# Second layer's weight conversions spread evenly over two tiles, and products with x's high parts before those with its low parts in a tile's first step

## The chip, the core and the metric

The kernel runs on one core of a Trainium2 chip. The metric is the device time of one execution in microseconds (us). Engines: PE is TensorE's matmul, PEld its weight load, DVE is VectorE, ACT is ScalarE, POOL is GpSimd, SP is SyncE, whose queue issues most DMAs.

## The reference

A delta-rule attention over 768 tokens (4 x 8 heads of 48) gives x, 3072 tokens of 384 features. Two feed-forward layers follow, and they are most of the work:

```python
x = attn_out.transpose(0, 2, 1, 3).reshape(3072, 384)
h = x @ w1_in                      # 384 -> 2048
g = h * (1 / (1 + exp(-1.702 * h)))
x = g @ w1_out                     # 2048 -> 384
h = maximum(x @ w2_in, 0)          # 384 -> 2048
out = (h * h) @ w2_out             # 2048 -> 384
```

The weights arrive as float64. The kernel turns them into float32 itself.

## The kernel before

**Tiles and steps.** Each layer runs over six tiles of 512 tokens; a tile is written here as (layer, j), from (1,0) to (2,5). In a tile, 16 steps f = 0 to 15 each take 128 of the 2048 hidden features. `step(ph, j, f)` issues the products into one of two PSUM banks h0 and h1 in turn, for three chunks c of x's 384 features, then ACT's tanh (or relu), DVE's product g, ACT's ghi and DVE's glo. `layer2` issues the products of the step before into three banks z0 to z2. So PE does nine 128x512 products into h and nine into z in a step.

**High and low parts.** PE works here on a float32r type, so every operand is a pair: hi, and lo = value - hi. A product is three: hi·hi, hi·lo and lo·hi. `split_x` makes x_hi on ACT and x_lo on DVE when a tile begins. Layer 1 has one pair of x buffers, so x_hi of tile j+1 may only be written when step 15 of tile j has been through its h products.

**Conversions.** `split_w` turns one chunk (128 x 384 float64, one f of one matrix) into hi and lo: ACT makes c0 from raw, DVE does two TENSOR_SCALAR into c1 (two buffers) and one SCALAR_TENSOR_TENSOR, ACT copies hi, and POOL subtracts lo = c1 - hi (`tt` with two queues: DVE where the planner finds it sooner). `load_w` brings the float64 into one of three raw buffers. The second layer has 32 chunks: 16 of w2_in into vi_hi and vi_lo, 16 of w2_out into wo_hi and wo_lo, in the place of the first layer's, so chunk f of those may only be written when `layer2` of (1,5) and f has been done.

**What sets the order.** `Program.add` records operations with costs; `flush` plans them with a cost table, engine by engine, and emits them in the planned order. From then on each engine runs its queue in order and waits on semaphores. There are two flushes: one up to the end of tile (1,4) with the attention, one for (1,5) and layer 2. In the attention, between the steps of layer 1, DVE also runs transposes (gu from G, kT_sb from gu), a product Td, and some fifteen small operations on 128x32 tiles named sm_.

Of the kernel before, what the change touches and what calls it, by code (L numbers as in the profile page):

```python
# [22 lines left out]
KX = 3  # L23
NF = DFF // 128
NT = B * S
CT = B * C
TT = 512
EPS = 1e-6
GATE = 1.702
TUNE = dict(  # L30
    fused=4,
    warm=(10, 6),
    burst=(6, 4, 220),
    blocks=(0, 1, 2, 3),
    ja=4,
    depth=2,
    half=8,
    slack=0.0,
# [12 lines left out]
class Program:  # L51
# [8 lines left out]
    def __init__(self, queues):  # L60
        self.queues = queues
        self.ops = []
        self.writer, self.readers = {}, {}
        self.free = {q: 0.0 for q in queues}
        self.dma_free = 0.0
        self.urgent = False
        self.columns = {}
        self.run = self.run_end = self.burst_end = 0.0

    def add(self, queue, cost, fn, reads=(), writes=(), early=0, nbytes=0, after=(), cold=None):  # L70
        n = len(self.ops)
        deps = set(after)
        for k in reads:
            if k in self.writer:
                deps.add(self.writer[k])
        for k in writes:
            if k in self.writer:
                deps.add(self.writer[k])
            deps.update(self.readers.get(k, ()))
        for k in reads:  # L80
            self.readers.setdefault(k, []).append(n)
        for k in writes:
            self.writer[k], self.readers[k] = n, []
        queue = (queue,) if isinstance(queue, str) else queue
        cost = cost if isinstance(cost, tuple) else (cost,)
        self.ops.append([queue, cost, fn, deps, n - early, nbytes, None, self.urgent, cold])
# [102 lines left out]
def kernel(  # L189
# [14 lines left out]
    w1_in, w1_out, w2_in, w2_out = (w.bitcast(I32) for w in (w1_in, w1_out, w2_in, w2_out))  # L204
    pg = Program({"pe": nc.tensor, "act": nc.scalar, "dve": nc.vector, "pool": nc.gpsimd, "sp": nc.sync})
# [8 lines left out]
    h_ps = [psum.tile([128, TT], F32, name=f"h{i}") for i in range(2)]  # L214
# [8 lines left out]
    wo_hi = main.tile([128, NF, DM], F32R, name="wo_hi")  # L223
    wo_lo = main.tile([128, NF, DM], F32R, name="wo_lo")
# [7 lines left out]
    NR = 3  # L232
# [33 lines left out]
    def act(n, reads, writes, early=0, **kw):  # L266
        kw.setdefault("func", AF.Copy)
        pg.add("act", c_act(n), lambda e: e.activation(**kw), reads, writes, early)  # L268
# [11 lines left out]
    def tt(n, reads, writes, out, in0, in1, op, queue="dve", early=0):  # L280
        cost = {"dve": c_dve(n), "pool": c_pool(n)}
        cost = cost[queue] if isinstance(queue, str) else tuple(cost[q] for q in queue)
        pg.add(queue, cost, lambda e: e.tensor_tensor(out=out, in0=in0, in1=in1, op=op), reads, writes, early)  # L283
# [5 lines left out]
    def stt(n, reads, writes, early=0, **kw):  # L289
        pg.add("dve", c_dve(n), lambda e: e.scalar_tensor_tensor(**kw), reads, writes, early)  # L290
# [4 lines left out]
    def mms(cost, todo, reads, writes, density=1.0):  # L295
        if not isinstance(cost, tuple):
            cost = cost, 2 * cost
        def fn(e):
            for out, lhsT, rhs, start, stop in todo:
                e.matmul(out=out, lhsT=lhsT, rhs=rhs, start=start, stop=stop)  # L300
        pg.add("pe", cost[0], fn, reads, writes, cold=(cost[1], 2400 * cost[0] * density))
# [4 lines left out]
    def load_w(src, f):  # L306
        s = n_conv[0] % NR
        n_conv[0] += 1
        dma(raw_sb[s], src[:, f].rearrange("p (n two) -> p n two", two=2), [], [("raw", s)], 128 * DM * 8)
# [27 lines left out]
    def halves_of(c0, n):  # L337
        return [x for x in range(2) if c0 <= x * CT < c0 + n]
# [362 lines left out]
    def layer2(ph, j, f, c0, n, hi, lo, K):  # L701
        for e in range(KX):
            ps = z_ps[e][:, c0:c0 + n]
            wh = wo_hi[:, f, 128 * e:128 * e + 128]
            wl = wo_lo[:, f, 128 * e:128 * e + 128]
            first, last = f == 0 and c0 == 0, f == NF - 1
            mms(3 * 0.000423 * n, [(ps, wh, hi, first, False), (ps, wh, lo, False, False), (ps, wl, hi, False, last)],
                [("wo", f, 0), ("wo", f, 1)] + K, [("z", e)])
        if f == NF - 1:
            dst = zd if ph == 1 else out  # L710
            for e in range(KX):
                key, zs = zs_of[ns[1] % NR]
                ns[1] += 1
                act(TT, [("z", e)], [key], out=zs, in_=z_ps[e], scale=0.5 if ph == 1 else 1.0)
                dma(dst[128 * e:128 * e + 128, TT * j:TT * j + TT], zs, [key],
                    [("zd", j, e)] if ph == 1 else [], 128 * TT * 4)

    def step(ph, j, f, c0=0, n=TT, b=0, mid=()):
        p = ns[0] % 2
        ns[0] += 1  # L720
        parts = range(2)
        if n == TT:
            ns[2] += ns[2] % 2
            s, o = ns[2] // 2 % NG, 0
            ns[2] += 2
        else:
            s, o = ns[2] // 2 % NG, CT * (ns[2] % 2)
            parts = [ns[2] % 2]
            ns[2] += 1
        W, halves = ("wi", "vi")[ph - 1], halves_of(c0, n)  # L730
        ps = h_ps[p][:, :n]
        for c in range(KX):
            wh = w_in_of[ph][0][:, f, 128 * c:128 * c + 128]
            wl = w_in_of[ph][1][:, f, 128 * c:128 * c + 128]
            hi, lo = x_hi[b][:, c, c0:c0 + n], x_lo[b][:, c, c0:c0 + n]
            mms(3 * 0.000423 * n, [(ps, wh, hi, c == 0, False), (ps, wh, lo, False, False), (ps, wl, hi, False, c == KX - 1)],
                [(W, f, 0), (W, f, 1)] + [("x", b, c, half, i) for half in halves for i in range(2)], [("h", p)])
        for todo in mid:
            todo()
        g, hi, lo = (x[s][:, o:o + n] for x in (g_sb, ghi_sb, glo_sb))  # L740
        kg, khi, klo = ([(x, s, i) for i in parts] for x in ("g", "ghi", "glo"))
        if ph == 1:
            act(n, [("h", p)], kg, out=g, in_=ps, func=AF.Tanh, scale=GATE / 2)
            stt(n, [("h", p)] + kg, kg, out=g, in0=g, scalar=1.0, in1=ps, op0=ALU.add, op1=ALU.mult)
        else:
            act(n, [("h", p)], kg, out=g, in_=ps, func=AF.Relu)
            tt(n, [("h", p)] + kg, kg, g, g, ps, ALU.mult)
        act(n, kg, khi, out=hi, in_=g)
        tt(n, kg + khi, klo, lo, g, hi, ALU.subtract)
        prev.append((ph, j, f, c0, n, hi, lo, khi + klo))  # L750
        while len(prev) > (1 if n == TT else TUNE["depth"]):
            layer2(*prev.pop(0))
# [5 lines left out]
    def convert(todo, load, n, key=None):  # L758
        for _ in range(n):
            if todo:  # L760
                _, key, f, hi, lo = todo.pop(0)
                split_w(key, f, hi, lo)
            if load:
                load_w(*(load[0][0], load.pop(0)[2]))

    with tc.manual_schedule():
# [111 lines left out]
        vi_hi = p2.tile([128, NF, DM], F32R, name="vi_hi")  # L878
        vi_lo = p2.tile([128, NF, DM], F32R, name="vi_lo")
# [6 lines left out]
        def load_z(j):  # L886
            for c in range(KX):
                dma(xf_sb[:, c], zd[128 * c:128 * c + 128, TT * j:TT * j + TT], [("zd", j, c)], xf_keys(c, 0, TT), 128 * TT * 4)

        w2i = [(w2_in, "vi", f, vi_hi, vi_lo) for f in range(NF)]  # L890
        w2o = [(w2_out, "wo", f, wo_hi, wo_lo) for f in range(NF)]
        ni, no = list(w2i), list(w2o)
        convert([], ni, NR)
        for f in range(NF):
            if f == 2:
                load_z(0)
            step(1, 5, f)
            convert(w2i, ni, 1)
        for key in [("x", 1, c, half, 1) for c in range(KX) for half in range(2)]:
            pg.readers[key] = [r for k in x_lo_keys for r in pg.readers.get(k, [])]  # L900
        split_x(1, 0, TT)
        while w2i:
            convert(w2i, ni, 1)
        for j in range(6):
            for f in range(NF):
                step(2, j, f, b=(j + 1) % 2)
                if j == 0:
                    if f == 0:
                        convert([], no, NR)
                    convert(w2o, no, 1)  # L910
                if f == 1 and j < 5:
                    load_z(j + 1)
                if f == 12 and j < 5:
                    split_x(j % 2, 0, TT)
# [69 lines left out]
```

## Time and profile before

| | us |
|---|---|
| median of 3 runs (lowest, highest) | 1086.88 (1084.77, 1090.79) |
| the profiled execution | 1084.37 |
| its span | 1082.7 |
| busy in it: PE, DVE, ACT, POOL | 1024.4, 589.6, 528.5, 332.9 |

The span runs from the first to the last instruction of the program in the profile; 1.7 us of the execution lie around it. Busy time of PE is a poor measure of its work, since matmuls overlap; the count of products in a stretch tells more. At full pace 128x512 products start 0.227 us apart. Layer 2 ends the span, and PE has no pause in most of it.

### The profile page before, as it was taken

The numbers are of one execution on the slowest core, as the hardware profiler recorded it, in microseconds if no ns is written. First come the engines' busy times: TensorE is split into PE (matmuls) and PEld (weight loads), VectorE is DVE, ScalarE is ACT, GpSimd is POOL, SyncE is SP. The second block draws the span as 40 slices with busy tenths as digits, with TensorE's granted clock in tenths as the row PEclk, the third lists the DMA queues.
The fourth block names the chain that finished last, engine by engine and source line by source line (L and its number), as shares of the span: only waits on it lengthen the run. The fifth ranks groups of instructions, "written<-read, shape, count | busy, mean of one in ns | idle before, by whom it ended". The sixth has DMA issues, their size and how long they took to land.

```text
span 1082.7 us, 23994 instructions
## 1 busy us (share of the span) xinstructions
PE 1024.4 (95%) x9900; PEld 832.9 (77%) x9900; DVE 589.6 (54%) x1122; ACT 528.5 (49%) x1088; POOL 332.9 (31%) x673
## 2 busy tenths in 40 slices
PE   4789899999999999999999989999999999999998
PEld 3778777867778787878788867788888888888886
DVE  6787886574655546453744799634333343433332
ACT  4586675636464546455544656534233242332323
POOL 1254251786647382847280144100000000000000
PEclk7798999999999999999999999999999999999999
DMA  8364462313223122212110566201001010000000
GB/s 225 98 170 133 139 174 61 113 31 93 57 60 101 60 56 88 64 51 73 50 34 5 172 179 169 94 0 59 1 7 53 1 59 1 1 30 1 30 1 29
DMA packets 43981, 76.32 MB, mean 70 GB/s; under 512 B 6624, under 2 KB 19552, under 8 KB 43872
## 3 DMA queue, kind: packets, MB, share of 16 engines
q1 hardware_dynamic: 43776, 74.75, 23.6%
q8 instruction: 77, 1.26, 0.5%
q14 instruction: 32, 0.26, 0.1%
q10 hardware_dynamic: 96, 0.05, 0.0%
HBM read 64.16 MB, written 9.44 MB: 68 GB/s over the span
## 4 chain that ended last, share of the span: by engine, by line
PE 66%; DVE 16%; ACT 8%; issue 4%; POOL 3%; DMA 2%; SPq 1%; DVEq 0%; ACTq 0%; POOLq 0%
PE h L300 28%; PE z L300 28%; PE a L300 9%; DVE c L287 3%; ACT G L273 3%; DVE kT_sb L293 2%; DVE glo L283 2%; DVE c L290 2%; DVE gu L293 1%; DVE g L290 1%; POOL tmpp L544 1%; DVE v_sb L283 1%; POOL U L547 1%; ACT gu L268 1%; DVE x_lo L283 1%
## 5 line engine op out<-in xcount | busy, mean ns | idle before, releaser
L268 ACT ACTIVATE g<-h 128x512 f32<-128x512 f32 (+1 forms) x200 | 115.5, 579 | 266.0 <-PE h L300 264.7
L300 PE MATMUL z<-glo,wo_hi 128*128 128x512 f32 (+1 forms) x600 | 231.8, 386 | 5.6 <-DVE glo L283 5.6
L300 PE MATMUL z<-ghi,wo_hi 128*128 128x512 f32 (+1 forms) x600 | 232.0, 387 | 0.1
L300 PE MATMUL z<-ghi,wo_lo 128*128 128x512 f32 (+1 forms) x600 | 229.7, 383 | 0.0
L283 DVE TENSOR_TENSOR glo<-g,ghi 128x512 fp32r<-128x512 f32 (+1 forms) x200 | 137.7, 689 | 98.6 <-ACT ghi L268 98.0
L268 ACT ACTIVATE ghi<-g 128x512 fp32r<-128x512 f32 (+1 forms) x200 | 122.6, 614 | 134.4 <-DVE g L290 68.5
L283 DVE TENSOR_TENSOR g<-g,h 128x512 f32<-128x512 f32 x96 | 66.1, 688 | 172.4 <-ACT g L268 172.4
L300 PE MATMUL h<-x_hi,wi_hi 128*128 128x512 f32 (+1 forms) x312 | 129.9, 416 | 18.3 <-DVE g L290 15.1
L544 POOL TENSOR_TENSOR tmpp<-U,gu 128x126 f32<-128x126 f32 (+22 forms) x248 | 113.2, 457 | 95.8 <-DVE U L287 77.0
L300 PEld LDWEIGHTS z<-glo,wo_hi 128*128 128x128 f32 x600 | 113.7, 189 | 33.2 <-DVE glo L283 11.8
L300 PEld LDWEIGHTS z<-ghi,wo_hi 128*128 128x128 f32 x600 | 113.6, 189 | 24.0 <-ACT ghi L268 0.9
L300 PEld LDWEIGHTS z<-ghi,wo_lo 128*128 128x128 f32 x600 | 113.7, 190 | 21.5
L290 DVE SCALAR_TENSOR_TENSOR g<-g,h 128x512 f32<-128x512 f32 (+1 forms) x104 | 66.5, 640 | 105.1 <-ACT g L268 104.9
L300 PE MATMUL h<-x_lo,wi_hi 128*128 128x512 f32 (+1 forms) x312 | 118.8, 381 | 3.2 <-DVE x_lo L283 3.2
L300 PE MATMUL h<-x_hi,wi_lo 128*128 128x512 f32 (+1 forms) x312 | 118.7, 380 | 0.4 <-DVE wi_lo L283 0.4
L300 PE MATMUL h<-x_hi,vi_hi 128*128 128x512 f32 x288 | 112.4, 390 | 0.8 <-PE h L300 0.8
L300 PE MATMUL h<-x_hi,vi_lo 128*128 128x512 f32 x288 | 112.2, 390 | 0.0
L547 POOL TENSOR_TENSOR U<-U,tmpp 128x126 f32<-128x126 f32 (+22 forms) x248 | 102.8, 415 | 20.4 <-DVE U L287 1.3
L300 PEld LDWEIGHTS h<-x_hi,wi_hi 128*128 128x128 f32 x312 | 59.7, 191 | 42.3 <-DVE g L290 24.7
L300 PEld LDWEIGHTS h<-x_hi,wi_lo 128*128 128x128 f32 x312 | 60.0, 192 | 11.6 <-DVE wi_lo L283 0.6
L300 PEld LDWEIGHTS h<-x_lo,wi_hi 128*128 128x128 f32 x312 | 60.1, 192 | 11.2 <-DVE x_lo L283 4.4
L273 ACT ACTIVATE ws<-a 32x384 f32<-32x384 f32 x92 | 44.3, 482 | 49.6 <-PE a L300 45.2
(117 smaller groups left out, 1451.4 us busy)
## 6 DMA issues: line engine op xcount, KB each, us to landing
raw<-in_w_in SPq DMA_DIRECT2D x32, 384.0 KB, 3.5
raw<-in_w_out SPq DMA_DIRECT2D x32, 384.0 KB, 3.4
kq<-in_kq SPq DMA_DIRECT2D x44, 256.0 KB, 3.0
kT_sb<-in_kq SPq DMA_DIRECT2D x11, 512.0 KB, 3.7
k_sb<-in_kt SPq DMA_DIRECT2D x12, 384.0 KB, 4.5
v_sb<-in_vt SPq DMA_DIRECT2D x12, 384.0 KB, 3.2
xf_sb<-zd SPq DMA_DIRECT2D x18, 256.0 KB, 2.7
out<-zs SPq DMA_DIRECT2D x18, 256.0 KB, 2.0
```

The source lines that it names most:

```text
L268: pg.add("act", c_act(n), lambda e: e.activation(**kw), reads, writes, early)
L273: e.activation(out=out, in_=in_, func=AF.Copy)
L283: pg.add(queue, cost, lambda e: e.tensor_tensor(out=out, in0=in0, in1=in1, op=op), reads, writes, early)
L287: pg.add("dve", c_dve(n, True), lambda e: e.tensor_scalar(**kw), reads, writes, early)
L290: pg.add("dve", c_dve(n), lambda e: e.scalar_tensor_tensor(**kw), reads, writes, early)
L293: pg.add("dve", c_dve(n), lambda e: e.transpose(out=out, in_=in_), reads, writes)
L300: e.matmul(out=out, lhsT=lhsT, rhs=rhs, start=start, stop=stop)
L544: e.tensor_tensor(out=t, in0=U[:, lo:hi, j:j + 1].to_broadcast(shape), in1=gu[:, j + 1:, j:j + 1].rearrange("p i o -> p o i").to_broadcast ...
L547: e.tensor_tensor(out=U[:, lo:hi, j + 1:], in0=U[:, lo:hi, j + 1:], in1=t, op=ALU.add)
```

## The change

Three edits. First, the lists of chunks: before, all 16 chunks of w2_in stood behind the steps of (1,5), one by one, and all 16 of w2_out behind those of (2,0). Now one list takes them in turns, vi 0, wo 0, vi 1, and so on. Second, a gate: chunk f of w2_in is held in the plan until step int(1.8 f), counted from the first step of (1,5), has been planned, that of w2_out two steps later. A gate is a dependency for the planner alone; it adds no wait on the chip. Third, in step 0 of the tiles (1,1) to (1,5) the six products with x_hi stand first, for all three chunks, and the three with x_lo after them, each as an operation of its own.

```diff
     def add(self, queue, cost, fn, reads=(), writes=(), ...):
         n = len(self.ops)
-        deps = set(after)
+        deps = set(after) | set(self.gate)
...
         for c in range(KX):
...
+            if ph == 1 and f == 0 and n == TT:
+                K = [("x", b, c, half, 0) for half in halves]
+                mms(2 * 0.000423 * n, [(ps, wh, hi, c == 0, False), (ps, wl, hi, False, False)], [(W, f, 0), (W, f, 1)] + K, [("h", p)])
+                late.append((c, wh, lo))
+                continue
...
+        for c, wh, lo in late:
+            mms(0.000423 * n, [(ps, wh, lo, False, c == KX - 1)], [(W, f, 0)] + [("x", b, c, half, 1) for half in halves], [("h", p)])
...
-        w2i = [(w2_in, "vi", f, vi_hi, vi_lo) for f in range(NF)]
-        w2o = [(w2_out, "wo", f, wo_hi, wo_lo) for f in range(NF)]
-        ni, no = list(w2i), list(w2o)
-        convert([], ni, NR)
+        w2 = [x for f in range(NF) for x in ((w2_in, "vi", f, vi_hi, vi_lo), (w2_out, "wo", f, wo_hi, wo_lo))]
+        w2_load = list(w2)
+        starts = []
+
+        def spread():
+            starts.append(len(pg.ops) - 1)
+            while w2:
+                at = int(TUNE["spread"] * w2[0][2]) + 2 * (w2[0][1] == "wo")
+                if at >= len(starts):
+                    break
+                pg.gate = starts[at:at + 1]
+                convert(w2, (), 1)
+                pg.gate = ()
+                convert((), w2_load, 1)
+
+        convert([], w2_load, NR)
         for f in range(NF):
             if f == 2:
                 load_z(0)
             step(1, 5, f)
-            convert(w2i, ni, 1)
+            spread()
...
-        while w2i:
-            convert(w2i, ni, 1)
         for j in range(6):
             for f in range(NF):
                 step(2, j, f, b=(j + 1) % 2)
                 if j == 0:
-                    if f == 0:
-                        convert([], no, NR)
-                    convert(w2o, no, 1)
+                    spread()
```

**DVE in the two tiles.** Names: g0, g1 and glo0, glo1 are the two buffers of a step's g and lo part, c10 and c11 the two buffers of a conversion, x_lo0 the low part of the next tile's x. Before, this stood for a step near the end of (1,5):

```order
L290 SCALAR_TENSOR_TENSOR g0_82<-g0_82,h0_67 128x512
L290 SCALAR_TENSOR_TENSOR c10_92<-c00_91,c10_92 128x384
L283 TENSOR_TENSOR glo0_86<-g0_82,ghi0_84 128x512
L287 TENSOR_SCALAR c11_93<-raw0_88 128x384 x2
L290 SCALAR_TENSOR_TENSOR c11_93<-c00_91,c11_93 128x384
L287 TENSOR_SCALAR c10_92<-raw1_89 128x384 x2
L290 SCALAR_TENSOR_TENSOR g1_83<-g1_83,h1_68 128x512
```

Two conversions lie between one g and the next. Now two conversions share two steps in most places, as here in (2,0):

```order
L285 TENSOR_TENSOR g1_83<-g1_83,h1_68 128x512
L289 TENSOR_SCALAR c11_93<-raw1_89 128x384
L285 TENSOR_TENSOR glo1_87<-g1_83,ghi1_85 128x512
L289 TENSOR_SCALAR c11_93<-raw1_89 128x384
L289 TENSOR_SCALAR c10_92<-raw2_90 128x384
L292 SCALAR_TENSOR_TENSOR c11_93<-c00_91,c11_93 128x384
L289 TENSOR_SCALAR c10_92<-raw2_90 128x384
L285 TENSOR_TENSOR g0_82<-g0_82,h0_67 128x512
L292 SCALAR_TENSOR_TENSOR c10_92<-c00_91,c10_92 128x384
L285 TENSOR_TENSOR glo0_86<-g0_82,ghi0_84 128x512
```

At six places the planner puts a whole pair between one glo and the next g, with a lo subtraction given to DVE (or a low part of x) among it; this one too is in (2,0):

```order
L285 TENSOR_TENSOR glo1_87<-g1_83,ghi1_85 128x512
L289 TENSOR_SCALAR c11_93<-raw0_88 128x384 x2
L289 TENSOR_SCALAR c10_92<-raw1_89 128x384
L292 SCALAR_TENSOR_TENSOR c11_93<-c00_91,c11_93 128x384
L289 TENSOR_SCALAR c10_92<-raw1_89 128x384
L285 TENSOR_TENSOR wo_lo_78<-c11_93,wo_hi_77 128x384
L292 SCALAR_TENSOR_TENSOR c10_92<-c00_91,c10_92 128x384
L285 TENSOR_TENSOR g0_82<-g0_82,h0_67 128x512
```

The last conversion now stands behind step 13 of (2,0); before, it stood behind step 0. Of the 32 subtractions DVE has nine, POOL 23; before it was three and 29.

**PE at the start of (1,4).** h0 is the bank of step 0, h1 that of step 15 before it and of step 1 after it. Before, from chunk 1 on:

```order
L300 MATMUL h0_67<-x_hi0_80,wi_hi_75 128x512
L300 MATMUL h0_67<-x_lo0_81,wi_hi_75 128x512
L300 MATMUL h0_67<-x_hi0_80,wi_lo_76 128x512
L300 MATMUL h1_68<-x_hi0_80,wi_hi_75 128x512
L300 MATMUL h1_68<-x_lo0_81,wi_hi_75 128x512
L300 MATMUL h1_68<-x_hi0_80,wi_lo_76 128x512
L300 MATMUL h0_67<-x_hi0_80,wi_hi_75 128x512
L300 MATMUL h0_67<-x_lo0_81,wi_hi_75 128x512
L300 MATMUL h0_67<-x_hi0_80,wi_lo_76 128x512
```

Now, from chunk 2 on (chunks 0 and 1 have had their two products):

```order
L302 MATMUL h0_67<-x_hi0_80,wi_hi_75 128x512
L302 MATMUL h0_67<-x_hi0_80,wi_lo_76 128x512
L302 MATMUL h1_68<-x_hi0_80,wi_hi_75 128x512
L302 MATMUL h1_68<-x_lo0_81,wi_hi_75 128x512
L302 MATMUL h1_68<-x_hi0_80,wi_lo_76 128x512
L302 MATMUL h0_67<-x_lo0_81,wi_hi_75 128x512
L302 MATMUL h1_68<-x_hi0_80,wi_hi_75 128x512
L302 MATMUL h1_68<-x_lo0_81,wi_hi_75 128x512
L302 MATMUL h1_68<-x_hi0_80,wi_lo_76 128x512
L302 MATMUL h0_67<-x_lo0_81,wi_hi_75 128x512
```

Six products of step 0 precede the first of step 1 in both; what follows is three products of step 0 in both, but now they are spread among those of step 1 and of z, and the last comes 11 products after the first of step 1, where it came five after it.

**DVE behind the start of (1,1).** sm_y, sm_a and sm_b are the attention's small tiles, g1 is step 1's product. Before:

```order
L287 TENSOR_SCALAR sm_y_120<-sm_y_120 128x32
L283 TENSOR_TENSOR sm_a_121<-sm_y_120 128x32
L290 SCALAR_TENSOR_TENSOR sm_b_122<-sm_a_121,gu1_108 128x32
L290 SCALAR_TENSOR_TENSOR sm_y_120<-sm_b_122,sm_y_120 128x32
L290 SCALAR_TENSOR_TENSOR g1_83<-g1_83,h1_68 128x512
```

Now:

```order
L289 TENSOR_SCALAR sm_y_120<-sm_y_120 128x32
L292 SCALAR_TENSOR_TENSOR g1_83<-g1_83,h1_68 128x512
L285 TENSOR_TENSOR sm_a_121<-sm_y_120 128x32
L292 SCALAR_TENSOR_TENSOR sm_b_122<-sm_a_121,gu1_108 128x32
L292 SCALAR_TENSOR_TENSOR sm_y_120<-sm_b_122,sm_y_120 128x32
```

Three small operations have gone behind g1 there. Behind the starts of (1,2), (1,3) and (1,4) it is the other way round: step 0's g stood right behind Td or the transpose of kT_sb and now stands behind Td and three to seven more of the small operations.

## Rows read from the trace of the kernel before

**Rows 1.** Busy time by stretch, with instructions counted; last columns clock, DMA share, GB/s.

```profile
600.00:620.00 20.00, 20.00 (x90) 16.52 (x89) 15.74 (x29) 14.79 (x29) 2.38 (x2) 1.00 0.56 158
620.00:700.00 80.00, 73.71 (x301) 54.75 (x300) 71.59 (x123) 47.87 (x94) 29.80 (x27) 1.00 0.53 153
700.00:780.00 80.00, 80.00 (x355) 66.28 (x354) 29.61 (x43) 27.40 (x46) 0.00 (x0) 1.00 0.06 20
```

**Rows 2.** PE's waits from 620 to 700 us: total, times, longest.

```profile
PE z L300 <- DVE glo L283: 2.9, 4, 0.8
PE h L300 <- DVE g L290: 2.1, 6, 0.6
```

**Rows 3.** DVE's groups by line and shape, 608 to 692 us.

```profile
L287 DVE TENSOR_SCALAR c<-raw 128x384 uint16<-128x384 uint16 x64 | 35.6, 603 | 0.0
L290 DVE SCALAR_TENSOR_TENSOR c<-c,c 128x384 int32<-128x384 int32 x32 | 21.9, 683 | 1.8 <-ACT c L268 0.2
L283 DVE TENSOR_TENSOR glo<-g,ghi 128x512 fp32r<-128x512 f32 x18 | 12.3, 683 | 1.7 <-ACT ghi L268 1.7
...
L283 DVE TENSOR_TENSOR vi_lo<-c,vi_hi 128x384 fp32r<-128x384 f32 x2 | 1.1, 560 | 1.2 <-ACT vi_hi L268 1.2
```

**Rows 4.** DVE's timeline in (1,5): start, length, instruction.

```profile
649.19 0.56 DVE L290 SCALAR_TENSOR_TENSOR c<-c,c 128x384 int32<-128x384 int32 x1
649.66 0.66 DVE L287 TENSOR_SCALAR c<-raw 128x384 uint16<-128x384 uint16 x2
...
652.33 1.47 DVE L287 TENSOR_SCALAR c<-raw 128x384 uint16<-128x384 uint16 x2
...
654.92 0.68 DVE L290 SCALAR_TENSOR_TENSOR g<-g,h 128x512 f32<-128x512 f32 x1
...
659.64 0.68 DVE L290 SCALAR_TENSOR_TENSOR g<-g,h 128x512 f32<-128x512 f32 x1
```

**Rows 5.** POOL's timeline at the same place.

```profile
652.44 1.11 POOL L283 TENSOR_TENSOR wo_lo<-c,wo_hi 128x384 fp32r<-128x384 f32 x1 [1.05 <-ACT wo_hi L268]
```

**Rows 6.** All engines' timeline in an undisturbed step of (2,0).

```profile
695.36 0.60 ACT L268 ACTIVATE g<-h 128x512 f32<-128x512 f32 x1 [2.09 <-PE h L300]
...
697.38 0.69 DVE L283 TENSOR_TENSOR glo<-g,ghi 128x512 fp32r<-128x512 f32 x1 [0.70 <-ACT ghi L268]
...
699.40 0.39 PE L300 MATMUL z<-glo,wo_hi 128*128 128x512 f32 x1
699.43 0.60 ACT L268 ACTIVATE g<-h 128x512 f32<-128x512 f32 x1 [2.09 <-PE h L300]
```

**Rows 7.** The page's part 6, one row: a DMA issue, KB, us to landing.

```profile
raw<-in_w_out SPq DMA_DIRECT2D x32, 384.0 KB, 3.4
```

**Rows 8.** PE's timeline at the start of (1,3).

```profile
419.92 0.49 PE L300 MATMUL h<-x_lo,wi_hi 128*128 128x512 f32 x1 [1.24 <-DVE x_lo L283]
...
421.12 0.51 PE L300 MATMUL h<-x_hi,wi_hi 128*128 128x512 f32 x1 [0.47 <-DVE g L290]
```

**Rows 9.** DVE's timeline there and behind it.

```profile
416.61 2.02 DVE L293 STREAM_TRANSPOSE gu<-G 128x1024 f32<-128x1024 f32 x1 [0.72 <-ACT G L273]
418.57 1.90 DVE L283 TENSOR_TENSOR x_lo<-xf_sb,x_hi 128x512 fp32r<-128x512 f32 x2
420.39 0.68 DVE L290 SCALAR_TENSOR_TENSOR g<-g,h 128x512 f32<-128x512 f32 x1
...
425.03 0.67 DVE L290 SCALAR_TENSOR_TENSOR g<-g,h 128x512 f32<-128x512 f32 x1
...
425.73 0.68 DVE L283 TENSOR_TENSOR Td<-kT_sb 128x512 f32<-128x512 f32 x1
```

**Rows 10.** PE's timeline behind the start of (1,1).

```profile
222.16 0.50 PE L300 MATMUL h<-x_hi,wi_hi 128*128 128x512 f32 x1 [2.19 <-DVE g L290]
```

**Rows 11.** DVE's timeline at the same place.

```profile
219.82 0.19 DVE L283 TENSOR_TENSOR sm_a<-sm_y 128x32 f32<-128x32 f32 x1
...
221.44 0.67 DVE L290 SCALAR_TENSOR_TENSOR g<-g,h 128x512 f32<-128x512 f32 x1
```

More of the change, by code (lines that the diff above doesn't have):

```diff
@@ L33 @@
     burst=(6, 4, 220),
+    spread=1.8,
     blocks=(0, 1, 2, 3),
@@ L67, in __init__ @@
         self.columns = {}
+        self.gate = ()
         self.run = self.run_end = self.burst_end = 0.0
@@ L730, in step @@
         W, halves = ("wi", "vi")[ph - 1], halves_of(c0, n)
-        ps = h_ps[p][:, :n]
+        ps, late = h_ps[p][:, :n], []
         for c in range(KX):
```

## The prediction

> **What bounds the kernel now.** The first view is busy time by stretch [rows 1]. From 700 us on, in layer 2, PE starts 355 products in 80 us and is never idle; there DVE is busy 29.61 of 80. From 620 to 700 us PE starts only 301, and DVE is busy 71.59 of 80. The 54 missing products, at 0.227 us each, are 12.3 us: that is what this stretch loses. Just before, from 600 to 620 us, DVE is already busy 15.74 of 20 and PE still starts 90, its full number. The clock column is 1.00 in all three, so it is not the clock. The second view says whom PE waits for in the lossy stretch: DVE's glo and DVE's g [rows 2]; the waits listed there are 5.0 us, and the rest of the loss is in matmuls that start late without a listed wait. The third view, DVE by group, says what DVE does instead: from 608 to 692 us, 64 TENSOR_SCALAR and 32 SCALAR_TENSOR_TENSOR of the conversions take 35.6 + 21.9 = 57.5 us [rows 3]. So all 32 conversions, of both matrices, fall into little more than the one tile (1,5). The list of the code says (1,5) and (2,0), but the planner takes a chunk of w2_out as soon as its place is free. In that tile DVE is the bound: from one g to the next it is 659.64 - 654.92 = 4.72 us [rows 4], where 18 products of PE need 18 x 0.227 = 4.09. That is 0.63 us lost per saturated step. Everywhere else in layer 2, PE is the bound, and what PE gains there the span gains.
>
> **The spread, in sum.** Two tiles give PE 32 x 4.09 = 131 us of work. DVE's work in them without conversions is 29.61/80 of that [rows 1], 48 us. The conversions add 57.5 us [rows 3], and the nine subtractions now on DVE 9 x 0.56 = 5.0 [rows 3]. That is 111 us of 131, 85%, where before it was above 100% of one tile. By the sum DVE is no longer the bound, and up to 12.3 us can be had.
>
> **The spread, step by step.** DVE runs in order, so a sum under 100% isn't enough. An undisturbed step shows the slack [rows 6]: tanh or relu starts at 695.36, glo ends at 697.38 + 0.69 = 698.07, and the first product that needs that glo starts at 699.40. So g and glo together may come 1.33 us late before PE waits. From the end of glo to the start of the next g there are 699.43 + 0.63 - 698.07 = 2.0 us, when I take g to start 0.63 after its ACTIVATE starts. In the common order (two conversions over two steps) there stand two to four TENSOR_SCALAR and one SCALAR_TENSOR_TENSOR in that gap. Two TENSOR_SCALAR take 0.66 when POOL is quiet, and 1.47 when POOL's subtraction runs beside them [rows 4, 5]; the SCALAR_TENSOR_TENSOR takes 0.47 up to the next start [rows 4]. That is 0.66 + 0.47 + 0.27 to 0.66, with one meeting with POOL (0.81) some 2.2 to 2.6 us: at most 0.6 late, inside 1.33. No stall there. At the six crowded places it is 2 x 0.66 + 2 x 0.47 + 0.56 = 2.8 us against 2.0 + 1.33 = 3.3. Without POOL it fits; with one meeting it is 3.6, a stall of 0.3. With two meetings, and a wait of about 0.7 for ACT's hi copy inside the gap, it is 5.1, a stall of 1.8. I take 0.4 for each place, nearer to the lower end since the saturated steps themselves lost 0.63: 6 x 0.4 = 2.4 us, with 0 and 6 x 1.8 = 10.7 as the ends. The gain left is 12.3 - 2.4 = 9.9 us.
>
> **Deadlines.** The last chunk of w2_in is now converted behind step 12 of (2,0) on DVE and needed at step 15, that of w2_out behind step 13 and needed after step 15: two to three steps, 8 to 12 us, where before it was nearly a whole tile. A transfer lands in 3.4 us [rows 7] and is issued some three conversions (11 us) ahead, so I cost this at nothing; if that cover fails, PE waits for weights in (2,0). The raw loads stand in SP's queue among loads of x and stores of z; none of those is needed sooner than half a tile after, and they cost nothing either.
>
> **High parts first.** The stall it aims at is at the start of (1,3), and alike at (1,2) and (1,4): PE waits for x_lo until 419.92, 1.24 us idle, then again for g until 421.12 [rows 8]. DVE's rows tell why: a transpose until 418.6, two x_lo until 420.47, then step 15's g until 421.07 [rows 9]. That g frees bank h1, which step 1's first product needs. DVE's order is still transpose, x_lo, g. Before 421.12 PE did two chunks of step 0, six products; now it will have done three pairs, also six. So the wait changes its name, from x_lo to g, and ends at the same time: gain nothing, or one product (0.23 us) at (1,2). What follows costs: the low products come last, spread over those of step 1 and z, and step 0's g, which stood at 425.03 [rows 9], now stands behind Td (0.68) and three to seven small operations of about 0.2: 1.3 to 2.1 us later. PE's work and the slack of 1.33 cover most of that; I take 0.4 per tile, 3 x 0.4 = 1.2 us lost. Behind (1,1), three small operations go behind step 1's g: it moves ahead by 221.44 - 219.82 = 1.62 us, and PE waits for just that g until 222.16, 2.19 us idle [rows 10, 11]. Since an ACT copy (ghi, 0.6 us) now comes in front of the copies that DVE's transpose there needs, 1.0 us is left. (1,5) starts with no stall to remove. Sum: 1.2 - 1.0 = 0.2 us, which I take as nothing; the ends are a gain of 3 (all x_lo stalls gone) and a loss of 4 (four tiles at 1 us).
>
> **The sum.** 1084.4 (profiled execution) - 9.9 = 1074.5 us. The median of the three runs is 2.5 us above the profiled execution, which puts the same change at 1077.0. I forecast between the two: **1075.5 us**. The forecast's own range is 1071 to 1079.
>
> **Rivals.**
> First, the order eats half: DVE at 85% in a fixed order has too little room, and the crowded places spread their delay to the steps around them. If half of the 32 steps lose 0.5 us, that is 8 of the 12.3, and the time is 1084 - 4 + 1 = 1081. For it: the crowded places lie close together early in (1,5) and in (2,0). Against it: 600 to 620 us, where DVE at 79% cost PE nothing [rows 1].
>
> Second, POOL meets glo. POOL's 23 subtractions run at other phases than before. In the lossy tile glo kept its length (mean 683 ns, as in undisturbed steps) while SCALAR_TENSOR_TENSOR of the conversions grew from 0.56 to 0.683 [rows 3, 4]: there POOL never fell on glo. If it now does at the crowded places, each stall grows by up to the subtraction's 1.11 us [rows 5]: 6 x 1.11 = 6.7, gain 3.2, time 1082. The Trainium skill (SBUF — State Buffer, section Who interferes with whom) states that a VectorE instruction with two SBUF inputs, which glo is, contends with a GpSimd instruction that reads SBUF, and that whoever issues first holds the port for the whole instruction. By that rule this rival is open at every step; the trace so far agrees for TENSOR_SCALAR (0.66 to 1.47) and shows no case for glo.
>
> Third, no gain: the plan's gate doesn't hold what it says, or conversions bunch again in (2,0), the DVE-bound stretch only moves, and the time stays within 4 us: 1083 to 1088. Against it is the emitted order, where the last conversion stands 13 steps later.
>
> Fourth, slower: bank h0. If step 0's g falls so far behind the attention's small operations that PE waits for bank h0 at step 2 of each tile start, four tiles lose; it decides the sign from 9.9/4 = 2.5 us per tile. The most that I find is 2.1 us of delay less the cover, so it needs more than the rows show: say 4 us, four times, 16 lost and 9.9 won, 1091.
>
> **Chances.** Forecast 0.66; first rival 0.13; second 0.08; third 0.09; fourth 0.04. A measurement of this kernel tells about 0.5%, 5.4 us, from no change, so faster means under 1081.4. The forecast's share and half of the first two rivals give faster 0.78; the other half, the third and a little of the fourth give same 0.18; slower 0.04. The range 1070.5 to 1083 leaves out the third and fourth, and the best case of all (12.3 and 3 won).
>
> **What would show it.** In the changed kernel's profile: busy DVE of about 0.85 through two tiles, none at 0.97; PE's count per 80 us at 350 or more through (1,5) and (2,0); conversions lying over some 125 us in place of 84; PE's waits for glo and g there under 3 us. At the starts of (1,2) to (1,4) PE's wait named x_lo is gone and one named g ends at the same distance from the transpose; the 2.19 us behind (1,1) shrinks to about 1.2. The forecast is wrong if DVE's glo or its conversions grow in mean length, if a product of (2,0) waits for vi or wo, or if PE's count from 200 to 600 us falls.

## The result, and the profile after

The changed kernel takes 1076.99 us (median of 8 runs, 1074.02 to 1081.45), the kernel before 1086.43 in the same comparison (8 runs, 1082.27 to 1090.79). The ratio is 0.9918, 95% interval [0.9891, 0.9945]: 9.4 us faster. The forecast was 1075.5.

**Stages instead of spans.** The span of the profiled execution fell from 1082.65 to 1072.29 us, 10.4 us, but 3.2 of these lie in the first 200 us. There all kernels of this document run DVE, ACT and POOL in the same order, and still their profiles differ by some microseconds (step 14 of (1,0) comes at 193.8 to 202.4 us, at a granted TensorE clock of 0.85 to 0.90 up to it). So here the span is cut at ACT's tanh or relu of certain steps (`g<-h`, 128x512): stage A runs from step 14 of (1,0) to step 14 of (1,4), stage B from there to step 0 of (2,1). Stage B holds all conversions of the second layer, and the granted clock is 1.00 (2.4 GHz) through it in every profile. It spans 34 steps, which at PE's full pace (4.08 us for the 18 products of a step) take 138.72 us; several kernels below take just that. Behind stage B every kernel needs 330.2 to 330.6 us. ACT's timeline (start, length, instruction) gives the ends of stage B, first in the kernel before, then in the changed one:

```profile
601.60 0.60 ACT L268 ACTIVATE g<-h 128x512 f32<-128x512 f32 x1
752.48 0.60 ACT L268 ACTIVATE g<-h 128x512 f32<-128x512 f32 x1 [2.10 <-PE h L300]
```

```profile
599.40 0.60 ACT L270 ACTIVATE g<-h 128x512 f32<-128x512 f32 x1
742.12 0.60 ACT L270 ACTIVATE g<-h 128x512 f32<-128x512 f32 x1 [2.09 <-PE h L302]
```

That is 150.88 us before and 142.72 after: 12.2 above the full pace, now 4.0. Stage A went from 404.54 to 405.58, but not at one clock (more on that below). So the gain lies in stage B, 8.2 us of it.

The windows of the changed kernel (columns as in [rows 1]: window, its length, busy time and count of PE, PEld, DVE, ACT, POOL, then clock, DMA share, GB/s):

```profile
600.00:620.00 20.00, 19.01 (x84) 15.38 (x84) 10.94 (x21) 11.34 (x21) 0.00 (x0) 1.00 0.33 99
620.00:700.00 80.00, 79.69 (x347) 64.49 (x346) 62.17 (x114) 46.02 (x88) 18.64 (x17) 1.00 0.48 138
700.00:780.00 80.00, 79.70 (x350) 65.17 (x349) 41.55 (x71) 34.70 (x62) 6.28 (x6) 1.00 0.17 51
608.00:739.00 131.00, 129.41 (x562) 104.48 (x561) 95.97 (x176) 73.58 (x140) 24.92 (x23) 1.00 0.39 114
```

PE starts 347 products where it started 301 [rows 1], at the same clock, and loses a few in (2,0), which it did not before. A new loss stands in the first window: 84 products for 90. PE's waits from 590 to 760 us (total, times, longest):

```profile
PE h L302 <- DVE g L292: 1.0, 1, 1.0
PE z L302 <- DVE glo L285: 0.4, 2, 0.2
```

Of the waits for glo [rows 2] 0.4 us is left; the one wait for g is that new loss. DVE's groups from 596 to 740 us (busy time, mean ns of one, idle time before):

```profile
L289 DVE TENSOR_SCALAR c<-raw 128x384 uint16<-128x384 uint16 x64 | 26.8, 461 | 2.2 <-POOL vi_lo L285 2.2
L285 DVE TENSOR_TENSOR glo<-g,ghi 128x512 fp32r<-128x512 f32 x34 | 24.0, 707 | 10.2 <-ACT ghi L270 9.5
L292 DVE SCALAR_TENSOR_TENSOR c<-c,c 128x384 int32<-128x384 int32 x32 | 22.5, 702 | 2.0 <-ACT c L270 1.0
```

The same 64 TENSOR_SCALAR that took 603 ns each [rows 3] take 461. The prediction moved them and left their length alone. That they got shorter was the first sign that something besides their number was at work.

### The profile page after: what moved, and what is told of

Its sections match the earlier page's. It is cut to its first block, busy times and chain, and to the rows that moved or that the text cites. A ratio compares the mean times of both kernels' runs of the same rounds, so it can differ in the third digit from the quotient of the medians.

```text
span 1072.3 us, 23979 instructions
## 1 busy us (share of the span) xinstructions
PE 1024.8 (96%) x9900; PEld 835.7 (78%) x9900; DVE 586.2 (55%) x1128; ACT 528.7 (49%) x1088; POOL 326.8 (30%) x667
## 4 chain that ended last, share of the span: by engine, by line
PE 65%; DVE 13%; POOL 9%; ACT 7%; issue 4%; DMA 1%; SPq 1%; ACTq 0%; DVEq 0%; POOLq 0%
PE h L302 28%; PE z L302 28%; PE a L302 9%; POOL tmpp L546 4%; POOL U L549 4%; ACT G L275 2%; DVE kT_sb L295 2%; DVE gu L295 2%; DVE g L292 1%; DVE glo L285 1%; DVE v_sb L285 1%; DVE c L292 1%; DVE c L289 1%; SPq L257 1%; DMA raw<-in_w_out 1%
## 5 line engine op out<-in xcount | busy, mean ns | idle before, releaser
L302 PEld LDWEIGHTS h<-x_hi,wi_lo 128*128 128x128 f32 x312 | 60.1, 193 | 11.4 <-DVE wi_lo L285 0.6
L275 ACT ACTIVATE G<-a 32x256 f32<-32x256 f32 (+1 forms) x172 | 55.3, 321 | 24.7 <-PE a L302 22.6
```

The costliest lines, as they stand in the source:

```text
L275: e.activation(out=out, in_=in_, func=AF.Copy)
```

## Experiments

"The spread" is edits one and two of the change, "high parts first" edit three.

**1. The spread without high parts first.**

```diff
-            if ph == 1 and f == 0 and n == TT:
+            if False:
```

> The spread of the conversions alone; step 0 of (1,1) to (1,5) as before the change. I compare two stretches: A from the tanh of step 14 of (1,0) to that of step 14 of (1,4) (before 404.5 us, changed kernel 405.6), B from there to the relu of step 0 of (2,1) (before 150.9, changed 142.7). Theory 1 (the spread gives all, high parts first costs some 1 us in A and 1 to 2 us in B): A 404.5, B 141 to 142, median 1074 to 1076. Theory 2 (high parts first helps, and the stall behind the start of (1,5) belongs to the spread): A 404.5, B 143 to 144, median 1077 to 1080.

Measured: 1072.5 us median, ratio to the kernel before 0.9892 [0.9871, 0.9913]. Stage A 404.17, stage B 140.67. The spread alone gives 10.2 us in stage B, all of the gain and more; 1.95 us above the full pace remain. Time and stage came out a little below theory 1's ranges. TENSOR_SCALAR took 461 ns here too.

**2. High parts first without the spread**: the kernel before with edit three alone.

```diff
+            if ph == 1 and f == 0 and n == TT:
+                K = [("x", b, c, half, 0) for half in halves]
...
+        for c, wh, lo in late:
```

> High parts first alone, in step 0 of (1,1) to (1,5); the lists of conversions as before. Theory 1: A 405.6, B 151 to 153, median 1087 to 1089, so no gain or a small loss. Theory 2 (the x_lo stalls of 3.1 us are gained): A 402 or less, B 150.9, median 1083.

Measured: 1083.53 us, ratio 0.9997 [0.998, 1.0014]; stage A 405.90, stage B 150.16, where theory 1 had 151 to 153. Edit three alone brings nothing that can be told from none.

**3. Both, but high parts first not in (1,5).**

```diff
-            if ph == 1 and f == 0 and n == TT:
+            if ph == 1 and f == 0 and n == TT and j < 5:
```

> The changed kernel with the old order of products in step 0 of (1,5) alone; (1,1) to (1,4) keep high parts first. Theory 1: the 1.15 us stall behind the start of (1,5) is gone; A 405.6, B 141 to 142, median 1076. Theory 2: the stall stays, A 405.6, B 142.7, median 1077.

Measured: 1074.95 us, ratio 0.9902 [0.9881, 0.9923]; stage A 406.43, stage B 140.63, that of the spread alone. So the 2.05 us by which the changed kernel's stage B is longer than that of experiment 1 come from the new order at the start of (1,5). What stands there, in the changed kernel's timelines of ACT, DVE and PE:

```profile
610.49 1.08 ACT L270 ACTIVATE g<-h 128x512 f32<-128x512 f32 x2
```

```profile
611.11 1.28 DVE L292 SCALAR_TENSOR_TENSOR g<-g,h 128x512 f32<-128x512 f32 x2 [5.02 <-ACT g L270]
```

```profile
611.85 0.50 PE L302 MATMUL h<-x_hi,wi_hi 128*128 128x512 f32 x1 [0.99 <-DVE g L292]
```

Step 0's low products now come last, so its tanh runs back to back with that of step 1 (one row, x2). Its g comes late, and step 2, which needs bank h0, waits 0.99 us. It is the wait that the fourth rival named, in the one tile where the prediction had looked for no cost, but not from that rival's cause: DVE was idle for 5.02 us before this g, so no other work of DVE held it back.

**4. The list in turns, without the gate.**

```diff
-                pg.gate = starts[at:at + 1]
```

> The changed kernel with the gate taken out of the plan: the operations of a conversion stand at the same place of the program, but the planner may pull them forward. Theory 1 (the loss is the bunching of conversions on DVE, and the gate is what prevents it): conversions end within about 85 us, DVE over 0.95 there, B 151 to 154, median 1086 to 1090. Rival (the turns of the two lists and the later place in the program suffice, or the stretch was not bound by DVE): B 143 to 145, median 1077 to 1080.

Measured: 1081.54 us, ratio 0.9974 [0.9958, 0.999]; stage B 148.11, TENSOR_SCALAR 548 ns, all of them within 84 us again. Time and stage lie between the two theories' ranges, so both missed: of the 8.2 us of gain 5.4 are gone and 2.8 are left. Most of it hangs on the distance between conversions, not on the two matrices taking turns; what keeps the 2.8 us was not tested.

**5 to 8. Who does the low subtractions.** Experiments 5 and 6 are the spread alone with all 32 subtractions of the second layer on POOL, then all on DVE; experiment 7 puts them all on DVE in the kernel before, without any spread; experiment 8 gates the spread at 1.0 steps in place of 1.8.

```diff
-    lo_both=99,
+    lo_both=32,
...
-           ("pool", "dve") if n_conv[1] <= TUNE["lo_both"] else "pool")
+           ("pool", "dve") if n_conv[1] <= TUNE["lo_both"] else "dve")
```

Experiment 5 has the first of these edits alone. Experiment 8:

```diff
-    spread=1.8,
+    spread=1.0,
```

> The spread alone (no change of the product order), with all 32 of the second layer's low subtractions planned on POOL, none on DVE. The stage from step 14's tanh of (1,4) to step 0's relu of (2,1) took 140.67 us with the spread alone, 1.95 above 34 steps at PE's full pace (138.72). Theory 1 (that rest is DVE's work at the crowded places, to which the subtractions on DVE belong): without them the stage takes 139 to 140 us and PE's waits for glo (0.4 us, twice) are gone. Rival (the rest is POOL holding back DVE's TENSOR_SCALAR): POOL runs nine subtractions more, the TENSOR_SCALAR get longer, and the stage takes 141 to 142. Second rival (the rest has another cause): 140.67 within 0.2. The whole time lies within 2 us of the spread alone, 1070.5 to 1074.5.

> The spread alone, with all 32 of the second layer's low subtractions on DVE and none on POOL. DVE gets 23 more at 0.56 us, 12.9 us, over 131 us of PE's work; if POOL no longer runs beside it, a TENSOR_SCALAR falls from about 0.46 to the 0.33 of an undisturbed pair's half, 64 x 0.13 = 8.3 us back. Theory 1 (DVE has room at this pace, and what counts is the crowd in single steps): stage 140 to 142 us, TENSOR_SCALAR at 0.33 to 0.36 each. Rival (DVE's room is used up, every microsecond added is lost): stage 143 to 146. Whole time 1070 to 1078.

> The kernel before, with all 32 low subtractions on DVE: conversions still bunched in (1,5), but POOL idle beside them. It measures how much of the bound tile was DVE's own work and how much POOL's interference. Before, the 64 TENSOR_SCALAR took 603 ns each. Theory 1 (DVE's own work bounds the tile; the interference is a part of it): TENSOR_SCALAR fall to 0.33 to 0.36, 64 x 0.26 = 16.6 us less, and 29 subtractions more are 16.2 us more, so the stage stays at 149 to 152 (150.88 before). Rival (POOL's interference is what costs; the subtractions on DVE find room): the stage falls to 144 to 147.

> The spread alone with 1.0 in place of 1.8 steps between chunks: chunk f of w2_in is held until step f, so all 32 conversions are gated into some 18 steps, two in each. DVE's work for a step without conversions is 29.61/80 of 4.09 = 1.5 us, and two conversions at 1.38 to 1.8 us each bring it to 4.3 to 5.1 us, above PE's 4.09. Theory 1 (what counts is how many conversions fall into a step's time): the conversions bunch as before, over 70 to 85 us, and the stage takes 147 to 151 us. Rival (the gain came from taking the two matrices in turns, or from the gate's mere presence): the stage takes 141 to 143.

Measured: experiment 5, 1077.35 us, ratio 0.9911 [0.9882, 0.9941], stage B 142.15; TENSOR_SCALAR stayed at 459 ns, but the conversions' SCALAR_TENSOR_TENSOR rose to 741 and glo to 731, and PE's waits for glo doubled to 0.8. So with nine more subtractions on POOL and none on DVE it got worse by 1.5 us, against theory 1 (and the first 200 us of its profiled execution took 202.4 us, at a granted clock of 0.85, where the others took 193.8 to 198.7 at 0.87 to 0.90, so its whole time missed the forecast by more). Experiment 6, 1072.96 us, ratio 0.9879 [0.9855, 0.9902], stage B 138.74: the full pace, below what either theory gave, with 12.9 us more work on DVE. Its window:

```profile
608.00:739.00 131.00, 131.00 (x579) 108.41 (x578) 97.01 (x202) 74.96 (x143) 0.00 (x0) 1.00 0.40 118
```

DVE is as busy as in the changed kernel (97.01 to 95.97), and PE never stops. Experiment 8: 1089.56 us in its only run, so without an interval; stage B 148.87, TENSOR_SCALAR 562 ns, as theory 1 had it, with 1.9 us in one wait of PE for a raw load. Its stage A (411.57) is an outlier: the granted clock was 0.95 in its first tile and 0.98 in two more. Experiment 7 turned the study: 1074.52 us, ratio 0.9892 [0.9852, 0.9932], stage B 138.75. The conversions are still bunched (first to last TENSOR_SCALAR 608.2 to 686.4 us, before 608.2 to 687.6), and the whole loss is gone, more than the rival had (144 to 147). Its groups on DVE from 608 to 692 us:

```profile
L287 DVE TENSOR_SCALAR c<-raw 128x384 uint16<-128x384 uint16 x64 | 22.5, 384 | 0.0
L290 DVE SCALAR_TENSOR_TENSOR c<-c,c 128x384 int32<-128x384 int32 x32 | 17.6, 550 | 0.2
...
L283 DVE TENSOR_TENSOR wo_lo<-c,wo_hi 128x384 fp32r<-128x384 f32 x16 | 8.8, 550 | 0.4 <-ACT wo_hi L268 0.4
L283 DVE TENSOR_TENSOR vi_lo<-c,vi_hi 128x384 fp32r<-128x384 f32 x16 | 8.8, 549 | 1.2 <-ACT vi_hi L268 1.2
```

My theory 1 there (DVE's own work bounds the tile) fell: with POOL idle, the work of the conversions and all the subtractions fit into one tile beside PE at full pace. The new theory is that POOL's subtraction holds DVE up. The rows of the kernel before, read again in the step of [rows 4], DVE first and then POOL:

```profile
655.51 1.01 DVE L290 SCALAR_TENSOR_TENSOR c<-c,c 128x384 int32<-128x384 int32 x1
656.44 0.68 DVE L283 TENSOR_TENSOR glo<-g,ghi 128x512 fp32r<-128x512 f32 x1
657.04 1.48 DVE L287 TENSOR_SCALAR c<-raw 128x384 uint16<-128x384 uint16 x2
```

```profile
655.10 1.00 POOL L283 TENSOR_TENSOR wo_lo<-c,wo_hi 128x384 fp32r<-128x384 f32 x1 [1.55 <-ACT wo_hi L268]
657.15 1.12 POOL L283 TENSOR_TENSOR wo_lo<-c,wo_hi 128x384 fp32r<-128x384 f32 x1 [1.05 <-ACT wo_hi L268]
```

POOL's first subtraction ends at 656.10. The SCALAR_TENSOR_TENSOR, which starts 0.41 us after that subtraction, ends at 656.52; it takes 1.01 us, where it takes 0.56 undisturbed. POOL's second ends at 658.27, and DVE's pair, 1.48 for 0.66, at 658.52. So a step of 4.72 us holds 0.45 + 0.82 = 1.27 us of being held up. Without these it would take 3.45, less than PE's 4.09, and DVE would not be the bound. But experiment 7 also changed the plan, so two more runs were needed.

**9. The kernel before, order untouched, POOL's subtractions cut to 8 columns.**

```diff
+        def fn(e):
+            w = 8 if narrow and e is nc.gpsimd else n
+            return e.tensor_tensor(out=out[..., :w], in0=in0[..., :w], in1=in1[..., :w], op=op)
```

> The kernel before, in its own order of instructions on every engine, but POOL's 29 low subtractions of the second layer work on 8 columns of the 384 (that part of the computation is left out, and PE reads other weights in place of vi_lo). The waits stay, POOL's time beside DVE goes. Theory 1, new since the run with the subtractions on DVE (the bound of the tile was POOL holding DVE up, not DVE's own work): with POOL quiet, two conversions are 2 x (0.54 + 0.47) us and g and glo 2 x 0.60, 3.2 us of DVE for a step of 4.09, so PE is not held up: the stage from (1,4) to (2,1) falls from 150.88 to 138.7 to 140 us and TENSOR_SCALAR from 603 ns to 0.38 us. Rival, the prediction's own reading (57.5 us of conversions in one tile are too much for DVE, whatever POOL does): the stage stays at 148 to 151. Second rival (the gain with the subtractions on DVE came from the other order that the planner made for it): also 148 to 151, with TENSOR_SCALAR at 0.38.

Measured: 1074.16 us, ratio 0.9892 [0.9853, 0.9932], stage B 138.72, the full pace to the hundredth. Windows, DVE's first two groups from 608 to 692 us, and POOL's:

```profile
620.00:700.00 80.00, 80.00 (x355) 66.24 (x354) 60.68 (x128) 50.46 (x99) 7.96 (x27) 1.00 0.52 154
700.00:780.00 80.00, 80.00 (x355) 66.24 (x354) 29.15 (x43) 27.95 (x46) 0.00 (x0) 1.00 0.06 20
```

```profile
L291 DVE TENSOR_SCALAR c<-raw 128x384 uint16<-128x384 uint16 x64 | 21.8, 386 | 0.2 <-DMA raw<-in_w_in 0.2
L294 DVE SCALAR_TENSOR_TENSOR c<-c,c 128x384 int32<-128x384 int32 x32 | 17.8, 556 | 2.8 <-ACT c L268 1.2
```

```profile
L286 POOL TENSOR_TENSOR wo_lo<-c,wo_hi 128x8 fp32r<-128x8 f32 x15 | 4.3, 289 | 32.4 <-ACT wo_hi L268 32.4
L286 POOL TENSOR_TENSOR vi_lo<-c,vi_hi 128x8 fp32r<-128x8 f32 x14 | 4.3, 306 | 73.4 <-ACT vi_hi L268 73.4
```

DVE runs the same instructions in the same order, two conversions in a step as before, and is busy 60.68 us of 80 where it was busy 71.59 [rows 1], while doing more steps. Both rivals fall: neither the amount of DVE's work nor its order made the loss. The shorter subtractions also make POOL's answer come sooner, and PE does not read vi_lo here, so a wait for POOL was not yet excluded. That is what the next run is for.

**10. Experiment 7 with a twin subtraction on POOL** that nobody reads. DVE and ACT run the same instructions in the same order as in experiment 7.

```diff
+        if n_conv[1] > 32:
+            tt(DM, [(key, f, 0)], ["twin"], twin[0], hi[:, f, :], hi[:, f, :], ALU.subtract, "pool")
```

> The kernel before with all 32 low subtractions on DVE (stage 138.75 us, 32 us of POOL time gone), and beside it POOL does a subtraction of the same size for each chunk, from the chunk's high part into a tile that nobody reads. DVE's order is that of the run without it, and nobody waits for POOL. Theory 1 (POOL's reading and writing beside DVE is what costs): each subtraction holds DVE up by 0.4 to 0.8 us as in the kernel before, 32 of them 13 to 26 us on an engine that had some 10 us free in the 80 us, so the stage rises to 143 to 152 us and TENSOR_SCALAR to 0.55 us or more. Rival (what cost was the wait for POOL, which held c1's buffers): stage 138.7 to 139.2.

Measured: 1083.82 us, ratio 0.9989 [0.9962, 1.0015], stage B 149.71: the loss is back, 11.0 us of it. DVE's groups from 608 to 692 us, and one meeting in the timelines of DVE and POOL:

```profile
L287 DVE TENSOR_SCALAR c<-raw 128x384 uint16<-128x384 uint16 x57 | 19.9, 380 | 0.0
L283 DVE TENSOR_TENSOR vi_lo<-c,vi_hi 128x384 fp32r<-128x384 f32 x16 | 16.7, 1041 | 1.2 <-ACT vi_hi L268 1.2
...
L283 DVE TENSOR_TENSOR wo_lo<-c,wo_hi 128x384 fp32r<-128x384 f32 x13 | 13.8, 1059 | 0.0
```

```profile
652.36 1.18 DVE L283 TENSOR_TENSOR vi_lo<-c,vi_hi 128x384 fp32r<-128x384 f32 x1
```

```profile
652.05 1.08 POOL L283 TENSOR_TENSOR twin<-vi_hi 128x384 fp32r<-128x384 f32 x1 [2.23 <-ACT vi_hi L268]
```

The price lands on other instructions than expected: TENSOR_SCALAR keeps 380 ns, and DVE's own subtractions, which ACT's high part releases at the same moment as the twin, rise from 0.55 to 1.04 and 1.06 us. They end 0.41 us after POOL's (653.54 and 653.13), as in the kernel before. PE's waits from 590 to 760 us name POOL for 0.4 us only; the rest is DVE's glo and g, 4.6 us. So the contention by itself, without a reader that waits, makes the loss.

**11. Subtractions on DVE, and high parts first in (1,1) alone.**

```diff
+            if ph == 1 and f == 0 and n == TT and j == 1:
```

> The kernel before with all 32 low subtractions on DVE, and the high parts first in tile (1,1) alone; no spread. In the four kernels with high parts first the time from step 14 of (1,0) to that of (1,1) was 105.9 to 106.5 us, in those without it 108.0 to 108.6 (one 112.8); from (1,3) to (1,4) it was 94.5 to 96.5 against 93.4 to 94.5. Theory 1 (the new product order gains at (1,1) and loses at (1,4) and (1,5)): 106 in the first tile, 93.4 in the fourth, 402.3 for the four; with 138.75 after them the whole is about 2.3 us below the run with the subtractions on DVE alone, 1071 to 1073. Rival (the 2.2 us come back as other waits in the next tiles): four tiles at 404.5, whole time 1073 to 1076.

Measured: 1074.15 us, ratio 0.9888 [0.9857, 0.9919]; stage B 138.75, stage A 408.19. Theory 1's 402.3 did not come, and the whole time lies in the rival's range: the tile to (1,1) took 107.14, a microsecond less than without the new order, and the next 102.81 in place of 100.5. But the granted clock was 1.00 in the first of the four tiles alone and 0.98 in the other three; in experiment 6 two tiles at 0.98 took 1.0 and 1.2 us longer than at 1.00. So this neither shows nor excludes that a gain at (1,1) is kept when the order is new there alone.

All kernels, in us and ns:

| kernel | POOL's subtractions | TENSOR_SCALAR ns | stage B | above 138.72 |
|---|---|---|---|---|
| before | 29, bunched | 603 | 150.88 | 12.2 |
| changed | 23, spread | 461 | 142.72 | 4.0 |
| 1 spread alone | 23, spread | 461 | 140.67 | 1.95 |
| 2 high parts first alone | 28, bunched | 566 | 150.16 | 11.4 |
| 3 not in (1,5) | 23, spread | 461 | 140.63 | 1.9 |
| 5 spread, all on POOL | 32, spread | 459 | 142.15 | 3.4 |
| 4 no gate | 27, bunched | 548 | 148.11 | 9.4 |
| 8 spread 1.0 | 30, bunched | 562 | 148.87 | 10.15 |
| 6 spread, all on DVE | none | 383 | 138.74 | 0.0 |
| 7 before, all on DVE | none | 384 | 138.75 | 0.0 |
| 9 before, 8 columns | 29, short | 386 | 138.72 | 0.0 |
| 10 all on DVE, twin on POOL | 32 twins, bunched | 380 (vi_lo 1041) | 149.71 | 11.0 |
| 11 all on DVE, (1,1) | none | 384 | 138.75 | 0.0 |

By the stage the best complete kernels are those with POOL quiet (6, 7 and 11; 7 is the kernel before with two edited lines). The medians of 6 and 7, 1072.96 and 1074.52, lie below that of the changed kernel, but the intervals of the ratios overlap, and experiment 1, with 1072.5, is not behind them; the stage, 4.0 us shorter than the changed kernel's and 1.9 shorter than that of experiment 1, is the surer sign.

## Why the prediction was right, and where not

**The time and its main term.** The spread was to gain 9.9 us in the two tiles, 12.3 of loss less a rest of 2.4. Alone it gained 10.2, with a rest of 1.95. High parts first took 2.05 of that back at (1,5), which leaves the 8.2 us of stage B.

**What bounds the tile: half read.** "In that tile DVE is the bound" holds: 4.72 us a step. But "what DVE does instead", 57.5 us of conversions, was put down as DVE's work. Against the same groups in experiment 7 it contained 35.6 - 22.5 = 13.1 us in TENSOR_SCALAR and 21.9 - 17.6 = 4.3 in SCALAR_TENSOR_TENSOR of being held up by POOL. The rows that say so were in the prediction (0.66 and 1.47, POOL's 1.11 beside it), and its second rival had the mechanism, but only as a price of the new places. It was not taken off the step of 4.72 to ask whether the tile would be bound without it. The Trainium skill (SBUF — State Buffer, section Who interferes with whom) states that a VectorE instruction with two SBUF inputs contends with a GpSimd instruction that reads SBUF, and that the one that comes second is blocked for the whole of the first. The SCALAR_TENSOR_TENSOR at 655 us and the subtraction at 652 us have two such inputs, came second and agree with it (1.01 us for 0.56 and 1.18 for 0.55). The prediction took TENSOR_SCALAR as its case, which has one SBUF input and is not what that sentence names; the case in its own rows was SCALAR_TENSOR_TENSOR, 0.56 grown to 0.683.

**The spread as a sum.** DVE's 111 us of 131, "85%", became 95.97, 73%: the conversions got shorter as they moved apart (57.5 to 49.3 us), and DVE's other work, put at 48, was some 42. In the traces 28 of POOL's 29 subtractions made a DVE instruction longer before, and 16 of 23 in the changed kernel; the others fall into DVE's pauses. Those that still meet DVE now have idle time behind them; how much of the gain is owed to each was not separated. It is a cure by dilution, as experiments 1, 4 and 8 show by degrees, and with POOL quiet there is nothing left to cure.

**Crowded places.** 2.4 us was forecast, 1.95 measured, but the terms were not six places at 0.4, so the near sum is in part luck: in experiment 1 PE's products start late around 665 us (0.6) and from 696 to 703 us (1.1), each time behind two pairs of TENSOR_SCALAR that POOL had held up to 1.48 or 1.49 us. It is all POOL: in experiment 6, with DVE's subtractions added to the crowd, it is 0.02. "Without POOL it fits" held. The second rival's meeting with glo took place at a small size: glo rose from 683 [rows 3] to 707 ns, and the conversions' SCALAR_TENSOR_TENSOR from 683 to 702. The prediction had named both as signs of being wrong; at this size they cost little (34 x 24 ns is 0.8 us of DVE).

**Deadlines and loads.** Costed at nothing, and PE waited for no weight and no load from 590 to 760 us in the changed kernel.

**High parts first.** "The wait changes its name" was right in part. PE's three waits for x_lo between 200 and 600 us (3.1 us) are gone, and the waits for g stay at 7.0 (7.5 before). But g takes over from x_lo only at (1,3); at (1,2) and (1,4) PE now waits for x_hi, ACT's part, 1.6 us in two waits, a name that the prediction did not have. Behind (1,1) the 2.19 us of [rows 10] became 1.31, where 1.2 was forecast. At (1,3), step 0's g now starts 6.58 us after the g that frees bank h1 (414.28 to 420.86), where it was 4.64 [rows 9]: 1.94 late, inside the forecast 1.3 to 2.1.

What this makes of stage A can be read only where the granted clock is the same. Its last tile in the kernel before, in experiment 4 (which has the new order in all five tiles) and in the changed kernel (columns as above, the clock third from the end):

```profile
508.18:601.60 93.42, 91.44 (x1045) 73.81 (x1044) 45.54 (x78) 46.24 (x93) 32.59 (x73) 1.00 0.14 44
506.52:601.05 94.53, 92.38 (x1045) 73.24 (x1044) 45.24 (x78) 46.22 (x92) 32.22 (x73) 1.00 0.14 44
502.89:599.40 96.51, 95.05 (x1045) 75.86 (x1044) 45.69 (x78) 45.91 (x92) 32.04 (x73) 0.96 0.14 43
```

In the changed kernel the granted clock was 0.50 (1.2 GHz in place of 2.4) for some 7 us from 515.5 us on, just after PE had stood idle for 1.0 us for x_hi; in experiment 4 it stayed at 1.00 after the same wait. So of the 3.1 us by which the changed kernel's tile is longer, 1.1 are the order's and 2.0 go with the clock. Experiment 4 kept a clock of 1.00 through all of stage A and took 404.25 us; the four kernels with the old order that did so too (before, 1, 7 and 10) took 404.17 to 404.67. Tile by tile experiment 4 stands at -1.9, +0.6, 0.0 and +1.1 us to their medians; forecast were -1.0 and three times +0.4. The sum, -0.2, is nothing, as forecast, from terms of another size and from one kernel; the first is reproduced (105.9 to 106.5 us in all four kernels with the new order in every tile of stage A). The step that failed is "(1,5) starts with no stall to remove": true, but the low products come last there too. It cost 2.05 us and was left out of the sum.

**What this means for the median.** The 8.2 us of stage B are the change's. In the profiled pair the first 200 us (-3.2) and stage A (+1.0) come to it; the first differ between kernels that run them in the same order, and the second had the lower clock in its last tile. The medians differ by 9.4 us; the interval of the ratio, 6.0 to 11.8 us, holds 8.2 as well. That the median came within 1.5 us of the forecast is helped by luck: 10.2 us were won by the spread and 2.05 lost at (1,5), a term that the sum didn't have, and the rest of the 9.4 lies outside stage B.

## What to carry to other kernels

When an engine looks like the bound, compare the mean length of its instructions there with the same instruction in a quiet place before its work is spread or cut: a longer one is waiting while it counts as busy. Moving work to a neighbour engine pays only if it doesn't hold up the one that it relieves; here a subtraction took DVE 0.55 us itself and cost it 0.45 to 0.82 when POOL did it. And an order of products that removes one wait is to be costed in every tile that it touches, those with no wait to remove too.

## What was not expected of the hardware

A DVE instruction that meets POOL's subtraction is not slowed in proportion but ends a fixed time after it: in the kernel before nine SCALAR_TENSOR_TENSOR of the conversions 0.41 or 0.42 us, eighteen TENSOR_SCALAR 0.24 to 0.26, and beside the twin 26 subtractions on DVE 0.41 or 0.42 again. And POOL's subtractions, 31 us in sum from 608 to 692 us on an engine that no wait of PE there names in the kernel before, cost the span 12 us.
